# Placing the rounding of the second MLP's weights and the splits of the experts' weights behind the steps they are traced in

## The chip, the cores and the metric

One core of a Trainium2 chip. The metric is the device time of one execution in microseconds (us); lower is better. The engines named below are TensorE (PE; its weight loads are PEld), VectorE (DVE), ScalarE (ACT), GpSimd (POOL) and SyncE (SP, which here only issues DMAs).

## The reference

Attention whose scores are factored, a mixture of experts over its output, and a second MLP over that. 8 x 576 = 4608 tokens of width 512; 8 experts of inner width 1024, two for each token; the second MLP has inner width 2048 and the activation h cos h.

```python
k_s = softmax(k, over the sequence); kv = einsum('bhsd,bhse->bhde', k_s, v)
x = einsum('bhsd,bhde->bhse', softmax(q, over d), kv)        # 4608 x 512
noisy = x @ w_gate + log1p(exp(x @ w_noise)) * noise
top2 of noisy per token, with softmax weights
y = sum over the two experts e of weight * (relu(x @ w1[e]) @ w2[e])
h = y @ w_in; out = ((h * cos(h)) @ w_out) as float32
```

The inputs w_in and w_out of the second MLP come as float64 and are handed to the kernel as pairs of 32-bit words.

## The kernel before

The kernel is written against a tile framework that traces instructions in program order and then orders each engine's queue by a simulation of its own: an instruction is queued when it is ready there, and earlier program order goes first among the ready ones. The engines run their queues strictly in that order. `tc.issue_after(ins)` adds an edge that is about order alone: what the block traces on the engine of `ins` stands behind `ins` in that engine's queue. Each `tc.If` (the block for an expert's tenth block of tokens, `last_block`, line 698) is ordered as one unit.

**Stages.** Attention runs in 36 columns of 128 tokens (`x_unit`); columns 18 to 35 stand in the second half of the main body and share their time with the routing (`routing`, in three chunks), the loading of expert 0's weights and, from column 26, the first groups of expert 0 (`early_group`). Then `experts()` (line 885) walks over `steps`, pairs of a token group g and a slice f of 128 inner columns. Expert 0 has groups of 2, 2, 2 and 3 blocks of 128 tokens (groups 0 to 2 are the early ones, group 3 the first in `experts()`), experts 1 to 7 groups of 4, 3 and 2 blocks, 8 slices each, so 24 steps; then come nine groups of 4 blocks with 16 slices for the second MLP.

**One step.** Matrix products are made in a split form, a = hi + lo, in three products. `mm1` (line 745) makes ph = x @ w1 for one slice; ScalarE writes hh, the rounded relu of ph, and VectorE hl = relu(ph) - hh (line 757). For the second MLP a chain of eight instructions takes the place of the relu (`times_cos`). `mm2`, LAG = 2 steps later, multiplies hh and hl with w2 into an accumulator per block. After a group's last slice the accumulators are copied to ys, even ones by ScalarE, odd ones by VectorE (line 787), and stored. The list `after` holds every hl in the order of tracing; `prep`, which transposes the next group's gathered rows on VectorE (line 677) and splits them into xh and xl (lines 680, 681), is already queued behind the hl of its step by it.

**Background work** is written as generators that are advanced by some steps at fixed places. `wbg` runs `w_load(e)` (line 125): 16 pieces of 128x512, of each a DMA into one of three buffers wst, a copy hi on ScalarE (line 136) and a subtraction lo on GpSimd (line 137); two sets of weights alternate. `cbg` runs `convert()` (line 810): 64 jobs, 32 for w_in and 32 for w_out, each of which loads 128x256 float64 numbers (line 844), makes float32 numbers of them by eight VectorE instructions (lines 821 to 825 as half1, 831 to 833 as half2) and stores them to DRAM (line 834), with two load buffers c64. It is added at the last step of group 3 and must be done by the end of expert 6, since expert 7's time loads the second MLP's first half. `nxt` is the next group, nx its blocks to prepare, p0 the step at which their preparation starts. A wait of SP, VectorE or another engine holds all that is behind it in its queue.

Of the kernel before, what the change touches and what calls it, by code (L numbers as in the profile page):

```python
# [10 lines left out]
F32 = mybir.dt.float32  # L11
# [16 lines left out]
def tile_attention_moe_moe2(  # L28
# [85 lines left out]
        return res  # L114

    W = [None, None]

    def alloc_w(pool, i):
        w1h = pool.tile([P, NK, F], F32R, name=f"w1h{i}")
# [5 lines left out]
    def w_load(e):  # L125

        pend = []
        w1h, w1l, w2h, w2l = W[e % 2]

        def split():  # L130
            (kind, i, fh, _), st = pend.pop(0)
            if kind == 0:
                hi, lo = w1h[:, i, fh * 512:(fh + 1) * 512], w1l[:, i, fh * 512:(fh + 1) * 512]
            else:
                hi, lo = w2h[:, i, :], w2l[:, i, :]
            nc.scalar.activation(hi, st, AF.Copy)  # L136
            nc.gpsimd.tensor_tensor(lo, st, hi.bitcast(F32), op=ALU.subtract)  # L137

        for pc in w_pieces(e):
            st = late[0].tile([P, 512], F32, name="wst", bufs=3)  # L140
            nc.sync.dma_start(st, pc[3])
            pend.append((pc, st))
            if len(pend) == 3:
                yield
                split()
        while pend:
            yield
            split()
# [209 lines left out]
    def x_t(n):  # L358

        t, c9 = divmod(n, PC)  # L360
        pt = ps_at("pqt", "tr", 2)
        for i in range(4):
            if c9 < 8:
                b, c = 2 * t + c9 // 4, c9 % 4
                src = QE[2 * b + i // 2][:, c, 2 * (i % 2):2 * (i % 2) + 2, :]
            else:
                src = QTL[t][:, 2 * i:2 * i + 2, :]
            nc.tensor.transpose(pt[:, i * P:(i + 1) * P], src.rearrange("p h d -> p (h d)"), ident)
        qtt = at.tile([P, 4, P], F32, name="qtt", bufs=2)
        nc.scalar.activation(qtt, pt.rearrange("p (i s) -> p i s", i=4), AF.Exp)  # L370
        QTT[n] = qtt

    def x_mm(n):
# [324 lines left out]
    def last_block(g):  # L698
# [4 lines left out]
        def up(f):  # L703
            fs = slice(f * P, (f + 1) * P)
            ph = ps_tr("ph")
            hh, hl = HH[f % (LAG + 1)][:, LASTB], HL[f % (LAG + 1)][:, LASTB]
            t = GB[f % 2][:, :P]
            if g.nb == 2:
                for kc in range(NK):
                    nc.tensor.matmul(ph[:, :2 * P], w1h[:, kc, fs], g.xh[:, kc, 2 * P:], start=kc == 0, stop=False)  # L710
                    nc.tensor.matmul(ph[:, :P], w1l[:, kc, fs], g.xh[:, kc, 2 * P:3 * P], start=False,
                                     stop=kc == NK - 1)
                nc.scalar.activation(t, ph[:, P:2 * P], AF.Copy)
                nc.vector.tensor_tensor(t, ph[:, :P], t, op=ALU.add)
            else:
                for kc in range(NK):
                    nc.tensor.matmul(ph[:, :P], w1h[:, kc, fs], g.xh[:, kc, LASTB], start=kc == 0, stop=False)
                    nc.tensor.matmul(ph[:, :P], w1h[:, kc, fs], g.xl[:, kc, LASTB], start=False, stop=False)
                    nc.tensor.matmul(ph[:, :P], w1l[:, kc, fs], g.xh[:, kc, LASTB], start=False, stop=kc == NK - 1)
                nc.vector.tensor_copy(t, ph[:, :P])  # L720
            nc.scalar.activation(hh, t, AF.Relu)
            nc.vector.scalar_tensor_tensor(hl, t, 0.0, hh.bitcast(F32), op0=ALU.max, op1=ALU.subtract)
            hs.append((hh, hl))
# [21 lines left out]
    def mm1(g, f):  # L745
# [7 lines left out]
        j = steps.index((g, f)) % (LAG + 1)  # L753
        hh, hl = HH[j][:, :g.N], HL[j][:, :g.N]
        if g.t is None:
            nc.scalar.activation(hh, ph, AF.Relu)  # L756
            after.append(nc.vector.scalar_tensor_tensor(hl, ph, 0.0, hh.bitcast(F32), op0=ALU.max, op1=ALU.subtract))  # L757
        else:
            kk = late[1].tile([P, 512], F32, name="kk", bufs=2)
            r = late[1].tile([P, 512], F32, name="r", bufs=2)  # L760
            times_cos(r, kk, ph)
            nc.scalar.activation(hh, r, AF.Copy)  # L762
            after.append(nc.vector.tensor_tensor(hl, r, hh.bitcast(F32), op=ALU.subtract))  # L763
        HT[g.i, f] = (hh, hl)

# [42 lines left out]
    EMAX = float(2 ** 16 * (1 + 7 / 8 - 2.0 ** -23))  # L808

    def convert():  # L810
        pend = []
        V = nc.vector

        def half1():
            src, t, dst = pend[0]
            v2 = t.rearrange("p (n w) -> p n w", w=2)
            lo, hi = v2[:, :, 0].bitcast(U32), v2[:, :, 1]
            ab = late[1].tile([P, CW], I32, name="ca", bufs=3)
            bits = late[1].tile([P, CW], I32, name="cb", bufs=1)

            V.tensor_single_scalar(ab, hi, 0x7fffffff, op=ALU.bitwise_and)
            V.tensor_scalar(ab.bitcast(F32), ab.bitcast(F32), EMIN, EMAX, op0=ALU.max, op1=ALU.min)
            V.tensor_scalar(bits, ab, 5, 2, op0=ALU.logical_shift_left, op1=ALU.logical_shift_right)
            V.scalar_tensor_tensor(bits, ab, 0x40000000, bits, op0=ALU.bitwise_and, op1=ALU.bitwise_or)
            V.scalar_tensor_tensor(bits, hi, -2 ** 31, bits, op0=ALU.bitwise_and, op1=ALU.bitwise_or)
            return lo, bits, ab

        def half2(lo, bits, ab):
            dst = pend.pop(0)[2]
            w = ab.bitcast(F32)  # L830
            V.tensor_single_scalar(ab, bits, -2 ** 23, op=ALU.bitwise_and)
            V.scalar_tensor_tensor(w, lo, 2.0 ** -52, w, op0=ALU.mult, op1=ALU.mult)
            V.tensor_tensor(w, w, bits.bitcast(F32), op=ALU.add)
            nc.sync.dma_start(dst, w)

        jobs = []
        for src, dst in ((w_in, wi_d), (w_out, wo_d)):
            s32 = src.bitcast(I32)
            for r in range(0, src.shape[0], P):
                for c in range(0, src.shape[1], CW):  # L840
                    jobs.append((s32[r:r + P, 2 * c:2 * (c + CW)], dst[r:r + P, c:c + CW]))
        for src, dst in jobs:
            t = late[1].tile([P, 2 * CW], I32, name="c64", bufs=2)
            nc.sync.dma_start(t, src)
            pend.append((src, t, dst))
            if len(pend) == 2:
                yield
                z = half1()
                yield
                half2(*z)  # L850
        yield
        half2(*half1())

    C2 = 2.0 * math.pi - C1
    MAGIC = 1.5 * 2.0 ** 23
# [29 lines left out]
    def experts():  # L885
# [4 lines left out]
        for i in range(first, len(steps) + LAG):  # L890
# [34 lines left out]
            if nxt is not None and f >= p0:  # L925
# [3 lines left out]
                next(pbg, None)  # L929
                if f == g.nf - 1:  # L930
                    finish(pbg)
            wbg.step(2 if g.t is not None or g.e == 0 else 1)
            if g.nb > 2 or f < p0:
                cbg.step(2 if f == 0 else 1)
            if f == g.nf - 1 and nxt is not None:
                if nxt.t == 0:
                    cbg.drain()
# [73 lines left out]
    for n in range(n, NCOL):  # L1011
# [10 lines left out]
                if t + 1 < NPAIR:  # L1022
                    load_tail(t + 1, "q")
        x_unit(n)
        wbg.step(4)
        if n >= 27:
            bg.step(2)
            dbg.step(1 + n % 2)
# [27 lines left out]
    left = 0  # L1056
    while dbg.q:
        dbg.step()
        left += 1
        if left >= 3:  # L1060
            next(pg, None)
# [93 lines left out]
```

## Time and profile before

| | us |
|---|---|
| median of 3 runs | 1932.73 |
| lowest and highest | 1931.42 and 1937.19 |
| the profiled execution | 1936.69 |
| its span, first to last instruction | 1934.6 |

| engine | busy us | share of the span |
|---|---|---|
| TensorE, matrix products | 1815.6 | 94% |
| TensorE, weight loads | 1531.3 | 79% |
| VectorE | 1118.6 | 58% |
| ScalarE | 860.6 | 44% |
| GpSimd | 447.7 | 23% |

The profile is of one execution. Times in it count from its first instruction; busy time is the union of an engine's instructions, and the granted clock is the share of full speed that TensorE was given. A wait names the engine and instruction that stood, and what ended the wait.

### The profile page before, as it was taken

The page shows a single profiled execution, that of the slowest core. Times are in us where ns is not written, and L with a number is a line of the kernel's source. Part 1 is how long each engine was busy: PE and PEld are TensorE (multiplying, and loading weights), DVE is VectorE, ACT ScalarE, POOL GpSimd, SP SyncE. Part 2 cuts the span into 40 slices and gives each one's busy share as a digit, 9 for nine tenths or more (in the row PEclk, how much of TensorE's full clock was granted, in tenths as well). Part 3 has the DMA queues.
Part 4 walks back from the last instruction along what each step waited for, and adds up shares of the span by engine and source line. Part 5 has one row for each costly group of instructions (what it writes and reads, how often), then busy time and mean ns, then how long its engine had stood idle before and what let it go on. Part 6 is the DMA issues. An engine that isn't in the chain of part 4 may idle for free. (4 is left out here: it accounts for less than half of the span.)

```text
span 1934.6 us, 27003 instructions
## 1 busy us (share of the span) xinstructions
PE 1815.6 (94%) x9738; PEld 1531.3 (79%) x9738; DVE 1118.6 (58%) x2138; ACT 860.6 (44%) x1514; POOL 447.7 (23%) x405
## 2 busy tenths in 40 slices
PE   5875988999899999999999999999999999999998
PEld 4764877788787788888888878888888888888886
DVE  4657677877767744334323357665656566665654
ACT  5542223313123132232424256666666666666654
POOL 6655033404114023041405143110101010110000
PEclk8775999999999999999999999999999999999999
DMA  9954246546545443252435342211212030201000
GB/s 269 291 168 129 79 128 206 186 142 192 150 125 182 141 132 115 79 155 81 133 92 148 98 139 65 71 28 60 56 33 66 23 88 16 72 28 49 1 23 23
DMA packets 179774, 206.18 MB, mean 107 GB/s; under 512 B 34224, under 2 KB 121264, under 8 KB 179632
## 3 DMA queue, kind: packets, MB, share of 16 engines
q1 hardware_dynamic: 160704, 152.17, 26.4%
q0 software_dynamic: 12160, 39.86, 7.1%
q10 hardware_dynamic: 6768, 12.32, 1.7%
q8 instruction: 82, 1.34, 0.3%
q14 instruction: 60, 0.49, 0.1%
HBM read 127.06 MB, written 49.43 MB: 91 GB/s over the span
## 5 line engine op out<-in xcount | busy, mean ns | idle before, releaser
L750 PE MATMUL ph<-xh,w1h 128*128 128x512 f32 (+2 forms) x1376 | 491.9, 357 | 6.9 <-DVE r L696 2.9
L752 PE MATMUL ph<-xh,w1l 128*128 128x512 f32 (+2 forms) x1376 | 491.3, 357 | 0.0
L751 PE MATMUL ph<-xl,w1h 128*128 128x512 f32 (+2 forms) x1376 | 490.6, 357 | 0.0
L774 PE MATMUL acc<-w2h,hh 128*128 128x512 f32 x1152 | 455.8, 396 | 17.1 <-DVE ys L787 9.7
L775 PE MATMUL acc<-w2l,hh 128*128 128x512 f32 x1152 | 453.3, 394 | 0.0
L776 PE MATMUL acc<-w2h,hl 128*128 128x512 f32 x1152 | 427.7, 396 | 21.5 <-DVE hl L757 19.7
L750 PEld LDWEIGHTS ph<-xh,w1h 128*128 128x128 f32 x1376 | 261.8, 190 | 47.1 <-DVE hl L757 4.0
L751 PEld LDWEIGHTS ph<-xl,w1h 128*128 128x128 f32 x1376 | 261.5, 190 | 38.2 <-DMA xl<-xg 0.8
L752 PEld LDWEIGHTS ph<-xh,w1l 128*128 128x128 f32 x1376 | 261.8, 190 | 32.1
L776 PEld LDWEIGHTS acc<-w2h,hl 128*128 128x128 f32 x1152 | 217.2, 190 | 73.7 <-DVE hl L757 26.1
L774 PEld LDWEIGHTS acc<-w2h,hh 128*128 128x128 f32 x1152 | 218.2, 189 | 65.7 <-ACT hh L756 11.1
L775 PEld LDWEIGHTS acc<-w2l,hh 128*128 128x128 f32 x1152 | 218.4, 190 | 40.4
L757 DVE SCALAR_TENSOR_TENSOR hl<-ph,hh 128x256 fp32r<-128x256 f32 (+2 forms) x200 | 107.1, 538 | 243.3 <-ACT hh L756 243.1
L756 ACT ACTIVATE hh<-ph 128x256 fp32r<-128x256 f32 (+2 forms) x200 | 93.9, 472 | 265.2 <-PE ph L752 250.8
L696 DVE SCALAR_TENSOR_TENSOR r<-r,ph 128x512 f32<-128x512 f32 x144 | 98.9, 687 | 151.4 <-ACT r L695 150.3
L618 POOL DMA_INDIRECT xg<-x_d,idx x80 | 76.8, 959 | 441.8 <-DVE xl L681 190.4
L694 ACT ACTIVATE r<-r 128x512 f32<-128x512 f32 x144 | 90.7, 630 | 151.9 <-DVE r L693 151.9
L763 DVE TENSOR_TENSOR hl<-r,hh 128x512 fp32r<-128x512 f32 x144 | 102.1, 709 | 86.4 <-ACT hh L762 86.3
L680 ACT ACTIVATE xh<-xg 128x512 fp32r<-128x512 f32 x106 | 66.7, 630 | 166.2 <-DVE xg L677 164.0
L137 POOL TENSOR_TENSOR w1l<-wst,w1h 128x512 fp32r<-128x512 f32 x80 | 104.9, 1326 | 137.9 <-ACT w1h L136 137.0
L618 POOL DMA_INDIRECT xg<-y_d,SL x36 | 34.3, 954 | 420.5 <-DVE xl L681 389.8
L692 DVE SCALAR_TENSOR_TENSOR r<-kk,ph 128x512 f32<-128x512 f32 x144 | 98.7, 685 | 51.6 <-ACT kk L691 50.0
(186 smaller groups left out, 2162.9 us busy)
## 6 DMA issues: line engine op xcount, KB each, us to landing
wst<-in_moe_w_dram SPq DMA_DIRECT2D x128, 256.0 KB
xl<-xg SPq DMA_DIRECT2D x396, 64.0 KB
y_d<-ys ACTq DMA_DIRECT2D x47, 256.0 KB
kt<-in_k_dram SPq DMA_DIRECT2D x16, 512.0 KB
vt<-in_v_dram SPq DMA_DIRECT2D x16, 512.0 KB
qt<-in_q_dram SPq DMA_DIRECT2D x16, 512.0 KB
x_d<-xs SPq DMA_DIRECT2D x32, 256.0 KB
c<-in_moe_w_in_dram SPq DMA_DIRECT2D x32, 256.0 KB
```

The costliest lines, as they stand in the source:

```text
L137: nc.gpsimd.tensor_tensor(lo, st, hi.bitcast(F32), op=ALU.subtract)
L618: return nc.gpsimd.indirect_dma_start(out=dst, out_offset=None, in_=src, in_offset=bass.IndirectOffsetOnAxis(ap=ix, axis=0))
L692: nc.vector.scalar_tensor_tensor(r, kk, -C1, ph, op0=ALU.mult, op1=ALU.add)
L696: nc.vector.scalar_tensor_tensor(r, r, 1.0, ph, op0=ALU.subtract, op1=ALU.mult, reverse0=True)
L750: nc.tensor.matmul(ph, w1h[:, kc, fs], g.xh[:, kc, :g.N], start=kc == 0, stop=False)
L751: nc.tensor.matmul(ph, w1h[:, kc, fs], g.xl[:, kc, :g.N], start=False, stop=False)
L752: nc.tensor.matmul(ph, w1l[:, kc, fs], g.xh[:, kc, :g.N], start=False, stop=kc == NK - 1)
L757: after.append(nc.vector.scalar_tensor_tensor(hl, ph, 0.0, hh.bitcast(F32), op0=ALU.max, op1=ALU.subtract))
L763: after.append(nc.vector.tensor_tensor(hl, r, hh.bitcast(F32), op=ALU.subtract))
L774: nc.tensor.matmul(g.acc[m], hh[:, ms], w2h[:, fr, :], start=f == 0, stop=False)
L775: nc.tensor.matmul(g.acc[m], hh[:, ms], w2l[:, fr, :], start=False, stop=False)
L776: nc.tensor.matmul(g.acc[m], hl[:, ms], w2h[:, fr, :], start=False, stop=f == g.nf - 1)
```

## The change

Rounding jobs are cut into four pairs of instructions, each queued behind the newest hl, with `cbg` stepping by pairs (1 to 3 a step) where it stepped by half jobs. Loads run three jobs ahead, the third buffer being GB[0], a gather buffer of the second MLP that is not yet in use; `last_block` keeps its scratch in GB[1] alone. A job's store is issued after the next job's first pair. The copy hi of a weight split is queued behind the newest entry of a new list `behind`: the hh of a step, or in the attention columns the exponential that writes qtt. Columns 18 and up advance `wbg` by 2 where they did by 4, steps of expert 0's group 3 by 1 where they did by 2, and the loop that finishes the early groups now advances it by 1.

```diff
--- before.py
+++ after.py
@@ -114,6 +114,7 @@
         return res
 
     W = [None, None]
+    behind = []
 
     def alloc_w(pool, i):
         w1h = pool.tile([P, NK, F], F32R, name=f"w1h{i}")
@@ -133,7 +134,9 @@
                 hi, lo = w1h[:, i, fh * 512:(fh + 1) * 512], w1l[:, i, fh * 512:(fh + 1) * 512]
             else:
                 hi, lo = w2h[:, i, :], w2l[:, i, :]
-            nc.scalar.activation(hi, st, AF.Copy)
+
+            with tc.issue_after(behind[-1].ins):
+                nc.scalar.activation(hi, st, AF.Copy)
             nc.gpsimd.tensor_tensor(lo, st, hi.bitcast(F32), op=ALU.subtract)
 
         for pc in w_pieces(e):
@@ -367,7 +370,7 @@
                 src = QTL[t][:, 2 * i:2 * i + 2, :]
             nc.tensor.transpose(pt[:, i * P:(i + 1) * P], src.rearrange("p h d -> p (h d)"), ident)
         qtt = at.tile([P, 4, P], F32, name="qtt", bufs=2)
-        nc.scalar.activation(qtt, pt.rearrange("p (i s) -> p i s", i=4), AF.Exp)
+        behind.append(nc.scalar.activation(qtt, pt.rearrange("p (i s) -> p i s", i=4), AF.Exp))
         QTT[n] = qtt
 
     def x_mm(n):
@@ -704,7 +707,7 @@
             fs = slice(f * P, (f + 1) * P)
             ph = ps_tr("ph")
             hh, hl = HH[f % (LAG + 1)][:, LASTB], HL[f % (LAG + 1)][:, LASTB]
-            t = GB[f % 2][:, :P]
+            t = GB[1][:, f % 2 * P:f % 2 * P + P]
             if g.nb == 2:
                 for kc in range(NK):
                     nc.tensor.matmul(ph[:, :2 * P], w1h[:, kc, fs], g.xh[:, kc, 2 * P:], start=kc == 0, stop=False)
@@ -753,13 +756,13 @@
         j = steps.index((g, f)) % (LAG + 1)
         hh, hl = HH[j][:, :g.N], HL[j][:, :g.N]
         if g.t is None:
-            nc.scalar.activation(hh, ph, AF.Relu)
+            behind.append(nc.scalar.activation(hh, ph, AF.Relu))
             after.append(nc.vector.scalar_tensor_tensor(hl, ph, 0.0, hh.bitcast(F32), op0=ALU.max, op1=ALU.subtract))
         else:
             kk = late[1].tile([P, 512], F32, name="kk", bufs=2)
             r = late[1].tile([P, 512], F32, name="r", bufs=2)
             times_cos(r, kk, ph)
-            nc.scalar.activation(hh, r, AF.Copy)
+            behind.append(nc.scalar.activation(hh, r, AF.Copy))
             after.append(nc.vector.tensor_tensor(hl, r, hh.bitcast(F32), op=ALU.subtract))
         HT[g.i, f] = (hh, hl)
 
@@ -808,48 +811,58 @@
     EMAX = float(2 ** 16 * (1 + 7 / 8 - 2.0 ** -23))
 
     def convert():
-        pend = []
         V = nc.vector
-
-        def half1():
-            src, t, dst = pend[0]
-            v2 = t.rearrange("p (n w) -> p n w", w=2)
-            lo, hi = v2[:, :, 0].bitcast(U32), v2[:, :, 1]
-            ab = late[1].tile([P, CW], I32, name="ca", bufs=3)
-            bits = late[1].tile([P, CW], I32, name="cb", bufs=1)
-
-            V.tensor_single_scalar(ab, hi, 0x7fffffff, op=ALU.bitwise_and)
-            V.tensor_scalar(ab.bitcast(F32), ab.bitcast(F32), EMIN, EMAX, op0=ALU.max, op1=ALU.min)
-            V.tensor_scalar(bits, ab, 5, 2, op0=ALU.logical_shift_left, op1=ALU.logical_shift_right)
-            V.scalar_tensor_tensor(bits, ab, 0x40000000, bits, op0=ALU.bitwise_and, op1=ALU.bitwise_or)
-            V.scalar_tensor_tensor(bits, hi, -2 ** 31, bits, op0=ALU.bitwise_and, op1=ALU.bitwise_or)
-            return lo, bits, ab
-
-        def half2(lo, bits, ab):
-            dst = pend.pop(0)[2]
-            w = ab.bitcast(F32)
-            V.tensor_single_scalar(ab, bits, -2 ** 23, op=ALU.bitwise_and)
-            V.scalar_tensor_tensor(w, lo, 2.0 ** -52, w, op0=ALU.mult, op1=ALU.mult)
-            V.tensor_tensor(w, w, bits.bitcast(F32), op=ALU.add)
-            nc.sync.dma_start(dst, w)
-
         jobs = []
         for src, dst in ((w_in, wi_d), (w_out, wo_d)):
             s32 = src.bitcast(I32)
             for r in range(0, src.shape[0], P):
                 for c in range(0, src.shape[1], CW):
                     jobs.append((s32[r:r + P, 2 * c:2 * (c + CW)], dst[r:r + P, c:c + CW]))
-        for src, dst in jobs:
-            t = late[1].tile([P, 2 * CW], I32, name="c64", bufs=2)
-            nc.sync.dma_start(t, src)
-            pend.append((src, t, dst))
-            if len(pend) == 2:
-                yield
-                z = half1()
-                yield
-                half2(*z)
-        yield
-        half2(*half1())
+        ring, loads, store = [], itertools.count(), None
+
+        def load():
+            n = next(loads)
+            if n < len(jobs):
+
+                t = GB[0].bitcast(I32) if n % 3 == 2 else late[1].tile([P, 2 * CW], I32, name="c64", bufs=2)
+                nc.sync.dma_start(t, jobs[n][0])
+                ring.append(t)
+
+        def held():
+
+            return tc.issue_after(after[-1].ins)
+
+        for _ in range(3):
+            load()
+        yield
+        for _, dst in jobs:
+            v2 = ring.pop(0).rearrange("p (n w) -> p n w", w=2)
+            lo, hi = v2[:, :, 0].bitcast(U32), v2[:, :, 1]
+            ab = late[1].tile([P, CW], I32, name="ca", bufs=3)
+            bits = late[1].tile([P, CW], I32, name="cb", bufs=1)
+            w = ab.bitcast(F32)
+
+            with held():
+                V.tensor_single_scalar(ab, hi, 0x7fffffff, op=ALU.bitwise_and)
+                V.tensor_scalar(w, w, EMIN, EMAX, op0=ALU.max, op1=ALU.min)
+            yield
+            if store is not None:
+                nc.sync.dma_start(*store)
+            with held():
+                V.tensor_scalar(bits, ab, 5, 2, op0=ALU.logical_shift_left, op1=ALU.logical_shift_right)
+                V.scalar_tensor_tensor(bits, ab, 0x40000000, bits, op0=ALU.bitwise_and, op1=ALU.bitwise_or)
+            yield
+            with held():
+                V.scalar_tensor_tensor(bits, hi, -2 ** 31, bits, op0=ALU.bitwise_and, op1=ALU.bitwise_or)
+                V.tensor_single_scalar(ab, bits, -2 ** 23, op=ALU.bitwise_and)
+            yield
+            with held():
+                V.scalar_tensor_tensor(w, lo, 2.0 ** -52, w, op0=ALU.mult, op1=ALU.mult)
+                V.tensor_tensor(w, w, bits.bitcast(F32), op=ALU.add)
+            store = (dst, w)
+            load()
+            yield
+        nc.sync.dma_start(*store)
 
     C2 = 2.0 * math.pi - C1
     MAGIC = 1.5 * 2.0 ** 23
@@ -929,9 +942,10 @@
                 next(pbg, None)
                 if f == g.nf - 1:
                     finish(pbg)
-            wbg.step(2 if g.t is not None or g.e == 0 else 1)
-            if g.nb > 2 or f < p0:
-                cbg.step(2 if f == 0 else 1)
+            wbg.step(2 if g.t is not None else 1)
+
+            busy = f < LAG or (nxt is not None and p0 <= f < p0 + nxt.nx)
+            cbg.step((1 if g.nb == 2 or f < LAG else 2) if busy else 2 if g.nb == 2 else 3)
             if f == g.nf - 1 and nxt is not None:
                 if nxt.t == 0:
                     cbg.drain()
@@ -1022,7 +1036,7 @@
                 if t + 1 < NPAIR:
                     load_tail(t + 1, "q")
         x_unit(n)
-        wbg.step(4)
+        wbg.step(2)
         if n >= 27:
             bg.step(2)
             dbg.step(1 + n % 2)
@@ -1056,6 +1070,7 @@
     left = 0
     while dbg.q:
         dbg.step()
+        wbg.step()
         left += 1
         if left >= 3:
             next(pg, None)
```

## Rows read from the trace of the kernel before

**Rows 1.** The page's busy time: engine, us, share of the span, instructions.

```profile
PE 1815.6 (94%) x9738; PEld 1531.3 (79%) x9738; DVE 1118.6 (58%) x2138; ACT 860.6 (44%) x1514; POOL 447.7 (23%) x405
```

**Rows 2.** Windows: stretch, length, busy PE PEld DVE ACT POOL, clock, DMA share, GB/s.

```profile
134.00:165.00 31.00, 12.71 (x119) 10.58 (x120) 17.96 (x55) 12.46 (x26) 22.73 (x18) 0.56 0.47 145
165.00:185.00 20.00, 14.29 (x99) 12.03 (x97) 19.66 (x50) 1.79 (x3) 7.29 (x6) 0.50 0.25 83
260.00:334.10 74.10, 61.87 (x332) 53.55 (x331) 55.96 (x110) 23.42 (x45) 33.17 (x29) 0.95 0.62 204
337.70:453.00 115.30, 106.11 (x506) 89.96 (x505) 88.14 (x191) 29.69 (x56) 29.69 (x25) 0.96 0.53 164
453.00:566.60 113.60, 104.18 (x502) 88.39 (x503) 87.09 (x191) 29.20 (x55) 30.22 (x26) 0.97 0.55 165
579.60:694.20 114.60, 105.07 (x506) 88.55 (x505) 82.43 (x188) 29.66 (x56) 29.55 (x25) 0.97 0.52 160
707.20:804.70 97.50, 97.50 (x496) 85.16 (x496) 34.99 (x49) 30.60 (x56) 29.12 (x26) 1.00 0.39 118
1130.00:1160.00 30.00, 25.67 (x101) 19.56 (x101) 13.75 (x16) 18.78 (x33) 19.28 (x17) 0.94 0.60 174
1720.00:1760.00 40.00, 40.00 (x178) 33.15 (x177) 27.78 (x42) 26.84 (x45) 6.08 (x6) 1.00 0.25 72
```

**Rows 3.** Waits, 337 to 694: total us, times, longest us.

```profile
PE acc L776 <- DVE hl L757: 14.6, 11, 2.2
...
PE acc L774 <- DVE ys L787: 9.7, 3, 3.7
```

**Rows 4.** Waits of PE, 260 to 334.1.

```profile
PE acc L776 <- DVE hl L757: 5.2, 2, 3.5
PE acc L774 <- ACT hh L756: 3.1, 3, 1.7
PE ph L750 <- DVE hl L757: 2.7, 3, 1.4
```

**Rows 5.** Waits, whole span, of a rounding job's first instruction.

```profile
DVE ca L821 <- DMA c<-in_moe_w_out_dram: 33.9, 23, 5.4
...
DVE ca L821 <- DMA c<-in_moe_w_in_dram: 29.6, 17, 5.6
```

**Rows 6.** Timeline of VectorE, 479 to 485: start, us, instruction.

```profile
479.66 3.31 DVE L824 SCALAR_TENSOR_TENSOR cb<-ca,cb 128x256 int32<-128x256 int32 x1
483.01 1.43 DVE L825 SCALAR_TENSOR_TENSOR cb<-c,cb 128x256 int32<-128x256 int32 x1
484.36 0.68 DVE L757 SCALAR_TENSOR_TENSOR hl<-ph,hh 128x512 fp32r<-128x512 f32 x1
```

**Rows 7.** Timeline of ScalarE, 479 to 485.

```profile
479.52 0.58 ACT L756 ACTIVATE hh<-ph 128x512 fp32r<-128x512 f32 x1
```

**Rows 8.** Timeline of GpSimd, 479 to 485.

```profile
480.15 1.29 POOL L137 TENSOR_TENSOR w1l<-wst,w1h 128x512 fp32r<-128x512 f32 x1
481.40 1.28 POOL L137 TENSOR_TENSOR w2l<-wst,w2h 128x512 fp32r<-128x512 f32 x1
```

**Rows 9.** Windows, line 821 alone: one instruction per rounding job.

```profile
260.00:334.10 74.10, 3.25 (x10) 0.95 0.62 204
453.00:566.60 113.60, 5.32 (x18) 0.97 0.55 165
```

**Rows 10.** Windows, line 757 alone: one hl per step, group of 3 blocks.

```profile
758.50:779.50 21.00, 2.79 (x5) 1.00 0.15 41
```

**Rows 11.** Instruction groups by line: count, busy us, mean ns.

```profile
L677 DVE STREAM_TRANSPOSE xg<-xl 128x512 f32<-128x512 f32 x99 | 110.7, 1118 | 0.0
...
L681 DVE TENSOR_TENSOR xl<-xg,xh 128x512 fp32r<-128x512 f32 x99 | 72.4, 732 | 30.7 <-ACT xh L680 30.4
```

**Rows 12.** Waits, 134 to 165.

```profile
PE pqt L368 <- ACT qtt L370: 16.5, 5, 4.9
```

**Rows 13.** Waits of SP's queue, 337 to 694.

```profile
SPq L844 <- DVE ca L832: 105.6, 31, 7.4
```

## The prediction

> **What bounds the kernel now.** The page comes first: TensorE is busy 94% of the span [rows 1], so only time in which it stands or runs slowly can be won. An average over the span hides where that is, so I cut it into windows at the branches of the conditional blocks, one window per expert [rows 2]. Seven lines matter. The three experts from 337.7 to 694.2 take 115.3, 113.6 and 114.6 us; the expert at 707.2 does the same 24 steps in 97.5 us with PE at 97.5 of 97.5 and full clock (the next three, not shown, agree within 0.1 us). The slow three differ from it in one thing: VectorE is busy 82 to 88 us there, 35 us in the clean one. That is the rounding of w_in and w_out, 18 of its 64 jobs in each slow expert [rows 9]. Together they lose 343.5 - 3 x 97.5 = 51.0 us, and their clock of 0.96 to 0.97 is inside that sum. Before them, from 260 to 334.1, PE stands 74.1 - 61.9 = 12.2 us, with ten jobs in the window [rows 2, 9].
>
> The waits say by what. In the slow experts PE waits 14.6 us for hl and 9.7 us for the copies ys of finished accumulators, both on VectorE [rows 3]; in 260 to 334.1 for hl 5.2 + 2.7 us and for hh 3.1 us [rows 4]. (The rest of the 51 us is the slow clock and PE's own stops behind those.) VectorE itself stood 33.9 + 29.6 = 63.5 us in front of the first instruction of a rounding job because its load had not landed [rows 5]; everything behind it in that queue stood too. The timeline shows the other half: hh was started at 479.52 and took 0.58 us [rows 7], but its hl ran at 484.36, after two rounding instructions of 3.31 and 1.43 us [rows 6]. So hl was ready to run for over 4 us and the queue order, not the data, held it.
>
> **Rounding behind hl, three buffers.** The work is unchanged: 64 jobs of 8 instructions. A job costs (88.14 - 34.99) / 18 = 2.95 us of VectorE, waits for GpSimd included [rows 2, 9]; a pair 0.74 us. What changes is place. Counted from the new step numbers, an expert takes 17 pairs in its group of 4 blocks, 17 in that of 3 and 10 in that of 2: 44 pairs, 11 jobs. The first two pairs come at the last step of group 3 and the last in expert 6's group of 3 blocks. So the 260 to 334.1 window loses all ten jobs, experts 1 to 3 go from 18 to 11 jobs, and experts 4 to 6, which are clean now, get 11 each.
>
> VectorE then has 35.0 + 11 x 2.95 = 67.5 us of work in 97.5 us, 69%. Is that a limit? By row, no: in 1720 to 1760 VectorE is busy 27.8 of 40 us, also 69%, and PE 40.0 of 40 at full clock [rows 2]. The load before was not only 76%: with the 63.5 us of load waits, about 1 us a job, some 18 us more per slow expert were blocked, 92%. A load that is two to three jobs ahead (a job every 8.9 us) has 18 us or more to land, while the longest wait for one was 5.6 us long; I cost those waits at nothing from now on.
>
> Locally it is tight. In the three middle steps of a group of 3 blocks VectorE has at most hl 0.68 [rows 6], one transposition and one xl, 1.12 + 0.73 [rows 11], and two pairs, 1.48: 4.0 us against a step of 21.0 / 5 = 4.2 us [rows 10]. If the one split of that step blocks the pair for a whole GpSimd instruction, 1.3 us [rows 8], it is 5.3 us, and three steps run 3.3 us late. LAG = 2 covers this: hl is read only two steps later, 8.4 us. Were that cover gone, 3.3 us would be lost in each of six experts. The ys copies have no such cover; they meet one pair at the first two steps. Bounds for the residue per expert: 0 (the 1720 row) and 17 (the slow experts); nearest is the row of equal load, so I take 2, six times 12 us.
>
> The DMAs: a load is now issued behind the fourth pair, a store behind the next job's first pair. Both are in SP's queue, where loads stood 105.6 us behind VectorE before [rows 13], with weight loads and the transposing transfers of xl behind them; with three buffers that wait moves to a later job, the longest was 7.4 us, and it is inside the 0 to 17. The new scratch place of the conditional block and GB[0] as third buffer add no instruction.
>
> **Splits behind hh or the exponential.** No instruction is added here either. A split's hi waits in ScalarE's queue behind the hh of its step; behind it are only copies for transposed blocks and ys; its lo holds back the gathers on GpSimd by up to one step, 5.4 us, once, which the next group's lead of three steps or more covers. In 260 to 334.1 the second expert's weights now come one piece a step, and the 3.1 us of waits for hh should go as well. I take 10 of the 12.2 us: the hl and hh waits without a little left for start-up.
>
> In the columns from 134 to 165 PE waited 16.5 us for the exponential [rows 12] and VectorE was busy 18.0 of 31.0 us, so up to 13.0 us could be won. But from 165 to 185 VectorE is the limit, 19.7 of 20 us [rows 2], with routing; and at two pieces a column about seven splits move into that stretch, where each may block routing for 1.3 us, 9 us. Bounds -13 and +9; nearer the middle, I take -3. At the hand-over to the second MLP, 1130 to 1160, PE stands 4.3 us; bounds -4 and +4, taken 0.
>
> **A rule against the change.** The row first: one rounding instruction took 3.31 us while GpSimd ran two splits back to back from 480.15 to 482.68 [rows 6, 8]. The Trainium skill, "SBUF — State Buffer", section "Who interferes with whom", says that GpSimd and VectorE share one pair of ports as an exclusive lock, so that one of the two blocks for the other's whole instruction. The trace agrees. By that rule a split and a pair released in the same step would collide each time; the rival on the slower side is that case.
>
> **Sum.** The profiled execution took 1936.69 us (span 1934.6 and 2.1 around it), 4.0 above the median of the runs. 1936.7 - 10 (260 to 334.1) - 51 (experts 1 to 3) + 12 (residue) - 3 (columns) = 1884.7; less the 4.0, **1881 us** for the median. 0.3% (6 us) is what a measurement can tell from no change.
>
> **Rivals.**
> - All of it goes: residue 0, columns -13, window -12.2: 1936.7 - 76.2 - 4.0 = 1856. For it: the 1720 row. Against: ys copies without cover. With it, up to a residue of 0.
> - Half comes back: residue 8 an expert, 48 us: 1917. For it: SP's queue still waits for VectorE, and the pairs sit in front of ys.
> - No change: the loss goes with jobs, not with their order. 64 jobs cost 61 us now and would cost 61 again: 1930. Against: the 4 us hold of a ready hl.
> - Slower: split against pair. If each of an expert's 16 splits meets a pair and holds it for its 1.3 us [rows 8], VectorE has 67.5 + 20.8 = 88.3 us, as many as the slow experts have, and all six lose 17: 1936.7 - 10 - 51 - 3 + 102 - 4.0 = 1971. It turns slower once an expert loses over 64 / 6 = 10.7 us. Against: the slow experts' 88 us contain the same 16 splits already, and their VectorE also stood for loads.
>
> **Chances.** Forecast 0.54, all 0.15, half 0.17, no change 0.06, slower 0.08. Faster 0.86, same 0.06, slower 0.08. The range from 1850 to 1926 leaves out the last two and little else.
>
> **What will show it.** No rounding instruction before the last step of group 3; first-of-job waits on the load near zero; experts 1 to 6 alike at 98 to 101 us, clock 1.00, VectorE near 67 us each; no PE wait on hl over 1 us; rounding until about 950 us. Wrong if experts 4 to 6 lose over 10 us each, if ys or hl still end PE's waits, if L833 still has instances of 3 us in numbers, or if the columns to 185 us take longer.

## The result and the profile after

The changed kernel takes 1875.22 us (median of four runs, 1874.38 to 1877.24) where the kernel before takes 1933.51 (four runs): a ratio of 0.9698 [0.9684, 0.9713], 3.0% faster. The forecast was 1881 and faster. The profiled execution took 1874.38 us and its span is 1872.4, so 62.2 us of the span went. The lines named here stand three further down in the changed kernel, up to the rounding: hl is L760, hh L759, the splits' hi and lo L139 and L140; the eight rounding instructions are L846, L847, L852, L853, L856, L857, L860 and L861.

The windows of the changed kernel, cut at the branches of the conditional blocks as in [rows 2] (length, then busy PE, PEld, DVE, ACT, POOL, granted clock, DMA share, GB/s):

```profile
134.00:165.00 31.00, 16.35 (x174) 13.45 (x172) 25.33 (x68) 10.57 (x23) 19.61 (x16) 0.66 0.41 120
165.00:185.00 20.00, 13.13 (x94) 11.03 (x95) 18.73 (x46) 4.47 (x9) 8.43 (x7) 0.59 0.34 110
250.00:318.60 68.60, 66.62 (x399) 59.26 (x396) 26.04 (x65) 22.50 (x46) 28.58 (x28) 1.00 0.49 156
321.20:419.40 98.20, 98.05 (x497) 85.24 (x497) 70.15 (x135) 30.96 (x58) 32.53 (x28) 1.00 0.57 172
422.00:519.60 97.60, 97.45 (x494) 84.85 (x494) 69.49 (x133) 29.32 (x55) 30.15 (x26) 1.00 0.51 159
534.60:632.20 97.60, 97.60 (x497) 85.20 (x496) 70.57 (x136) 29.92 (x56) 30.00 (x26) 1.00 0.51 158
647.10:744.80 97.70, 97.70 (x498) 85.29 (x497) 70.69 (x136) 29.92 (x56) 30.00 (x26) 1.00 0.51 158
872.30:969.80 97.50, 97.50 (x496) 85.14 (x496) 63.57 (x119) 29.82 (x56) 30.06 (x26) 1.00 0.47 145
```

The third row ends where expert 1's first conditional block starts; it has no rounding in it. The next five are experts 1, 2, 3, 4 and 6. The first three were 115.3, 113.6 and 114.6 us; all five are now what only the clean experts were, with PE busy in nearly the whole stretch at a granted clock of 1.00 while VectorE is busy about 70 us (63.6 in expert 6), twice the 35 us of the clean expert of before.

Where the 62.2 us went, from the branch that ends a stretch to the one that ends the next, profiled execution against profiled execution:

| stretch | before, us | after, us | difference |
|---|---|---|---|
| columns, up to the early groups' hl | | | -1.1 |
| from there to the end of group 3 | | | -14.4 |
| both: start to the end of group 3 | 334.1 | 318.6 | -15.5 |
| experts 1, 2, 3 | 118.1, 114.4, 114.5 | 100.8, 100.2, 97.6 | -48.5 |
| the two conditional blocks behind experts 1 to 3 in which PE works | 13.0, 13.0 (26.0 together) | 14.9, 14.9 (29.9 together) | +3.9 |
| second MLP, last branch to the end | 804.6 | 802.4 | -2.2 |

These make -62.3; experts 4 to 6 differ by 0.1 us in all.

Now the waits. In the whole stretch from 321 to 970, experts 1 to 6, TensorE's matrix products have no row at all among the waits; its weight loads have three (us in total, times, longest):

```profile
PEld acc L779 <- issue: 0.5, 1, 0.5
PEld acc L779 <- DVE cb L853: 0.5, 1, 0.5
PEld ph L754 <- issue: 0.5, 2, 0.3
```

The 14.6 us for hl and the 9.7 us for ys of [rows 3] have no successor. What stands is VectorE, in the same stretch:

```profile
DVE hl L760 <- ACT hh L759: 151.5, 107, 5.8
DVE gb L717 <- ACT gb L716: 27.9, 20, 3.7
...
DVE ys L790 <- PE acc L779: 5.4, 11, 1.0
```

The sign has turned round: hl used to be ready and stand behind rounding; now VectorE has finished its background work and stands 107 times at hl, waiting for hh. No wait for a rounding load is left among VectorE's rows. Such idle time costs nothing: VectorE is off the path.

One step as it now runs, VectorE from 442.9, then ScalarE and GpSimd (start, us, instruction; idle time before it in brackets):

```profile
442.98 0.69 DVE L760 SCALAR_TENSOR_TENSOR hl<-ph,hh 128x512 fp32r<-128x512 f32 x1 [1.96 <-ACT hh L759]
443.59 1.11 DVE L680 STREAM_TRANSPOSE xg<-xl 128x512 f32<-128x512 f32 x1
444.61 0.44 DVE L852 TENSOR_SCALAR cb<-ca 128x256 int32<-128x256 int32 x1
445.08 0.43 DVE L853 SCALAR_TENSOR_TENSOR cb<-ca,cb 128x256 int32<-128x256 int32 x1
```

```profile
442.35 0.60 ACT L759 ACTIVATE hh<-ph 128x512 fp32r<-128x512 f32 x1 [2.47 <-PE ph L755]
442.84 0.62 ACT L139 ACTIVATE w1h<-wst 128x512 fp32r<-128x512 f32 x1
```

```profile
443.60 1.30 POOL L140 TENSOR_TENSOR w1l<-wst,w1h 128x512 fp32r<-128x512 f32 x1 [1.35 <-DMA wi_d<-ca]
```

VectorE waits 1.96 us and runs hl 0.03 us after hh has ended at 442.95. Then come a transposition and a rounding pair. The split's copy hi stands behind the hh of its step, so GpSimd's one subtraction starts after hl is nearly done.

That spacing shows in the rounding as well, here in an instruction with two inputs (L824 before, L853 after) and one with one input (L831, L857). First the kernel before, then the changed one (shortest/median/longest ns, first and last start):

```profile
L824 DVE SCALAR_TENSOR_TENSOR cb<-ca,cb x64: 370/426/3314, 265.8 to 692.6; 128x256 int32<-128x256 int32 x64
L831 DVE TENSOR_SCALAR ca<-cb x64: 252/289/4440, 267.1 to 694.0; 128x256 int32<-128x256 int32 x64
```

```profile
L853 DVE SCALAR_TENSOR_TENSOR cb<-ca,cb x64: 417/426/1399, 321.3 to 945.7; 128x256 int32<-128x256 int32 x64
L857 DVE TENSOR_SCALAR ca<-cb x64: 280/294/296, 328.0 to 947.6; 128x256 int32<-128x256 int32 x64
```

The medians are the same within 5 ns; the instances of 3 to 4 us are gone (for the 3.31 us, [rows 8] show two splits in a row). The longest, 1.40 us, is about one split. Collisions have not become fewer: 34 of the 512 rounding instructions took over 0.6 us before, up to 4.44 us, and 60 do now, up to 1.40 us, each beside a split; what has changed is that none lasts longer than about one split, and that they stand behind hl. The rounding is spread from 318 to 949 us instead of 265 to 707.

### The profile page after: what moved, and what is told of

Read it like the earlier page. It is cut to its first block, busy times and chain, and to the rows that moved or that the text cites. A ratio compares the mean times of both kernels' runs of the same rounds, so it can differ in the third digit from the quotient of the medians.

```text
span 1872.4 us, 27040 instructions
## 1 busy us (share of the span) xinstructions
PE 1798.1 (96%) x9738; PEld 1525.2 (81%) x9738; DVE 1136.9 (61%) x2138; ACT 857.8 (46%) x1514; POOL 452.4 (24%) x405
## 5 line engine op out<-in xcount | busy, mean ns | idle before, releaser
L779 PE MATMUL acc<-w2h,hl 128*128 128x512 f32 x1152 | 422.1, 391 | 0.6
L759 ACT ACTIVATE hh<-ph 128x256 fp32r<-128x256 f32 (+2 forms) x200 | 95.6, 478 | 392.2 <-PE ph L755 387.6
L760 DVE SCALAR_TENSOR_TENSOR hl<-ph,hh 128x256 fp32r<-128x256 f32 (+2 forms) x200 | 108.1, 541 | 247.0 <-ACT hh L759 238.7
L140 POOL TENSOR_TENSOR w1l<-wst,w1h 128x512 fp32r<-128x512 f32 x80 | 106.1, 1329 | 258.0 <-ACT w1h L139 241.5
L140 POOL TENSOR_TENSOR w2l<-wst,w2h 128x512 fp32r<-128x512 f32 x80 | 106.6, 1337 | 134.2 <-ACT w2h L139 106.2
```

What stands on the lines that cost most here:

```text
L779: nc.tensor.matmul(g.acc[m], hl[:, ms], w2h[:, fr, :], start=False, stop=f == g.nf - 1)
```

## The experiments

Theory A: what the 51 us of experts 1 to 3 cost was order alone, hl and ys standing behind rounding in VectorE's queue, and the order edge removes it whatever the load. The rivals: the load (18 jobs an expert against 11, so density), the waits for the loads (so the third buffer), the splits' collisions. Each kernel was timed beside the kernel before; ratios carry their 95% interval.

### The two parts apart

rounding_alone keeps the new `convert`, its pace and buffers, and frees the splits again:

```diff
-            with tc.issue_after(behind[-1].ins):
-                nc.scalar.activation(hi, st, AF.Copy)
+            nc.scalar.activation(hi, st, AF.Copy)
...
-            wbg.step(2 if g.t is not None else 1)
+            wbg.step(2 if g.t is not None or g.e == 0 else 1)
...
-        wbg.step(2)
+        wbg.step(4)
...
-        wbg.step()
```

> The changed kernel with the rounding's part alone: pairs behind hl, three buffers, the new pace; the splits are free again, 4 a column, 2 a step in expert 0, none in the loop that finishes the early groups. Theory A, order: it is the rounding ahead of a ready hl that stopped TensorE, so experts 1 to 6 stay at 97.5 to 98.5 us and nearly all of the 58 us is here: 1875 to 1883 us, the rest being what the splits do before expert 1. Theory B, the splits count as much: free copies on ScalarE that wait for their load hold hh, so experts 1 to 3 are at 101 us or more and the total is 1890 us or more.

Measured: 1883.36 us, 0.9736 [0.9718, 0.9755]. Expert 1 in it:

```profile
325.00:423.10 98.10, 97.95 (x498) 85.12 (x497) 66.00 (x133) 30.17 (x56) 30.26 (x26) 1.00 0.49 159
```

Clean: nearly all of the gain is the rounding part.

splits_alone is the other half: `convert`, its pace and the conditional block's scratch of before, with the splits held and their new pace.

> The kernel before with the splits' part alone: hi behind hh or the exponential, 2 a column, 1 a step in expert 0 and in the loop that finishes the early groups. The rounding is as before. Theory A, order of the rounding: experts 1 to 3 keep losing 14 us or more each, total 1922 to 1936 us. Theory B: hh comes sooner and hl with it, experts 1 to 3 win 5 us or more each, total 1915 us or less.

Measured: 1944.39 us, 1.0047 [1.003, 1.0065]: slower by half a per cent, outside of what was expected. (Its profiled execution, 1937.89 us, is the fastest of five, so its rows show less than the median lost.) Its experts 1 and 2, and PE's first wait from 328 to 570 (9.1 us from 337 to 580 before):

```profile
327.50:448.20 120.70, 107.87 (x505) 90.31 (x505) 90.40 (x181) 29.99 (x58) 32.96 (x28) 0.94 0.50 160
450.40:569.60 119.20, 105.69 (x500) 89.08 (x501) 96.55 (x198) 27.70 (x55) 29.17 (x25) 0.96 0.50 159
```

```profile
PE acc L779 <- DVE hl L760: 23.2, 12, 4.7
```

The early part gained 9.8 of the 15.5 us that the whole change gains there (expert 1 starts at 324.3 instead of 334.1), and the three experts then lost more than that, 14 us. So beyond the early part the splits' edge gained nothing while hl still stood behind rounding.

### The hold, the pace and the buffers

no_hold is the changed kernel without the rounding's order edge alone:

```diff
         def held():
-            return tc.issue_after(after[-1].ins)
+            return ExitStack()
```

> The changed kernel with the pairs traced at the same steps and with three buffers, but with no order edge behind hl, so that the ordering may queue them as soon as they are ready. Theory A, order: pairs are queued ahead of hl again and packed into the first experts, whose windows go back to 108 us or more: total 1915 to 1935 us. Rival, pace and buffers: the three buffers and the finer steps are what helped; waits for loads stay near zero, experts stay under 101 us, total 1875 to 1890 us.

Measured: 1928.78 us, 0.9963 [0.995, 0.9976]. Windows of its experts 1 and 2 and PE's waits from 326 to 570:

```profile
326.00:447.70 121.70, 107.32 (x505) 89.60 (x504) 97.08 (x204) 29.70 (x58) 32.63 (x28) 0.94 0.54 170
450.00:568.50 118.50, 104.34 (x501) 87.77 (x501) 100.10 (x213) 28.23 (x55) 29.66 (x25) 0.97 0.53 168
```

```profile
PE acc L779 <- DVE hl L760: 24.4, 14, 4.4
PE acc L777 <- DVE ys L790: 3.0, 1, 3.0
```

With loads three jobs ahead and pairs in place of halves, VectorE stood 2.3 us for a load in that stretch (and 24.9 us for stores), and these two experts lost as much as ever. So neither the buffer nor the cut does it.

three_pairs_a_step keeps the hold and packs the work: `cbg.step(3)` in every step, 17, 18 and 17 jobs in experts 1 to 3, nearly as many as before.

> The changed kernel with three pairs at every step, so 18 jobs an expert as in the kernel before, and rounding done within the first four experts; pairs still behind hl, three buffers. VectorE then has about 35 + 18 x 3.2 = 93 us of work in 97.5 us. Theory A, order: hl goes ahead and LAG covers the rest, experts 1 to 3 at 100 us or less, total within 8 us of the changed kernel, 1875 to 1883. Rival, density: what helped is that only 11 jobs fall into an expert; with 18 the windows go back to 108 us or more and the total to 1905 us or more.

Measured: 1874.77 us, 0.9691 [0.9673, 0.9708], as the changed kernel. Its experts 1 to 3:

```profile
321.00:419.80 98.80, 98.65 (x500) 85.78 (x499) 80.68 (x179) 30.51 (x58) 32.47 (x27) 1.00 0.61 194
422.00:520.60 98.60, 98.60 (x499) 85.95 (x500) 83.09 (x187) 28.86 (x55) 30.05 (x25) 1.00 0.60 189
534.20:632.40 98.20, 98.20 (x500) 85.69 (x499) 84.66 (x188) 29.64 (x56) 29.95 (x25) 1.00 0.60 190
```

VectorE is busy up to 84.66 of 98.20 us, 86%, and PE does not stop. In [rows 2] it was busy 76% and PE lost 17 us. Density falls as a rival.

hold_alone is the kernel before with one edge around each half of a job and nothing else:

```diff
+            mark = tc.issue_after(after[-1].ins)
+            mark.__enter__()
             V.tensor_single_scalar(ab, hi, 0x7fffffff, op=ALU.bitwise_and)
...
+            mark.__exit__(None, None, None)
             return lo, bits, ab
...
+            mark = tc.issue_after(after[-1].ins)
+            mark.__enter__()
             V.tensor_single_scalar(ab, bits, -2 ** 23, op=ALU.bitwise_and)
...
+            mark.__exit__(None, None, None)
             nc.sync.dma_start(dst, w)
```

> The kernel before with one thing added: each half of a rounding job (five instructions, three instructions) is queued behind the newest hl. Two load buffers, the old pace of 22 halves an expert, free splits. Theory A, the order edge is the gain: experts 1 to 6 at 97.5 to 100 us, the total that of the rounding's part alone, 1878 to 1890 us. Rival, the cut into pairs and the third buffer carry it: halves of 1.8 us in front of the next hl and jobs that wait for loads in the queue, experts at 103 us or more, 1900 us or more.

Measured: 1882.53 us, 0.9735 [0.972, 0.975], the same as rounding_alone. The edge alone makes the whole of the rounding part's gain, with two buffers, halves and the old pace. That pace was in the program all along: the rounding ran ahead of it, as early as its loads allowed, 18 jobs an expert and done by 707, and behind hl it falls back to 11 jobs an expert and runs until 948 (no_hold, where nothing keeps it, has 21 in experts 1 and 2 each). VectorE's waits for the loads, 57.8 us from 321 to 707 before, shrink to this one row:

```profile
DVE ca L823 <- DMA c<-in_moe_w_in_dram: 0.7, 1, 0.7
```

They were a result of that running ahead. What they cost by themselves while hl stood behind them, no run separates from the order.

two_buffers takes the third buffer from the changed kernel:

```diff
-                t = GB[0].bitcast(I32) if n % 3 == 2 else late[1].tile([P, 2 * CW], I32, name="c64", bufs=2)
+                t = late[1].tile([P, 2 * CW], I32, name="c64", bufs=2)
...
-        for _ in range(3):
+        for _ in range(2):
             load()
```

> The changed kernel with two load buffers in place of three, loads two jobs ahead. Theory A, order: an expert has 11 jobs, one in about 9 us, and a load lands in time or its wait stands behind hl where nothing waits for it; 1873 to 1880 us. Rival, loads: about 1 us of wait a job comes back and stands in VectorE's queue ahead of the next hl and of ys, experts at 101 us or more, 1890 us or more.

Measured: 1873.73 us, 0.9684 [0.9669, 0.9699]: the buffer is worth nothing.

edges_only is hold_alone with the splits' edge added, the paces of before:

```diff
+    behind = []
...
-            nc.scalar.activation(hi, st, AF.Copy)
+            with tc.issue_after(behind[-1].ins):
+                nc.scalar.activation(hi, st, AF.Copy)
...
```

> The kernel before with the two order edges and nothing else: rounding halves behind the newest hl, splits' hi behind hh or the exponential. Two buffers, halves, the old places and numbers of steps for both. Theory A, order is the whole change: 1871 to 1879 us, as the changed kernel. Rival: the splits' new step numbers (2 a column, one a step in expert 0, and in the loop that finishes the early groups) are part of it; then expert 1 starts later than in the changed kernel and the total stays at 1880 us or more.

Measured: 1877.74 us, 0.971 [0.969, 0.973]. Two order edges make about 56 of the 58 us that the medians differ by.

### The columns

columns_4 goes back to four splits a column, `wbg.step(4)`, held as in the change.

> The changed kernel with four splits a column, still behind the exponential, so that they are done by column 22, before the routing's VectorE work. If the splits that fall into the routing are what gave back the 8.6 us that the columns had won by column 22, the columns end 3 to 6 us earlier: 1869 to 1873 us. If splits in front of the next exponential wait for their loads as before, the win by column 22 is gone and the total is 1875 to 1880 us.

Measured: 1878.84 us (1873.99 to 1881.82), 0.9713 [0.9699, 0.9726]; its interval overlaps that of the changed kernel, and the 3 to 6 us that the first expectation hoped for did not come. From 134 to 170 PE waits for the exponential nearly as long as before the change [rows 12]:

```profile
PE pqt L371 <- ACT qtt L373: 12.9, 5, 4.8
```

columns_gap moves the splits instead: three a column up to column 20, none from 21 to 25, then two, `wbg.step(3 if n < 21 else 0 if n < 26 else 2)`.

> The changed kernel with three splits a column up to column 20, none from 21 to 25, where the routing's first chunk keeps VectorE busy, and two a column after. If splits on GpSimd in that stretch hold the routing's VectorE instructions, early groups start 3 to 7 us earlier and so does the end: 1868 to 1872 us. If the routing itself is the limit there, nothing moves: 1873 to 1877 us.

Measured: 1874.47 us (1866.97 to 1878.12), 0.9683 [0.966, 0.9707]. From column 23 to 28 the columns run 7 to 8 us ahead of the kernel before (6 us ahead of the changed kernel at column 28), and by columns 32 to 35 only 0.6 to 2.2 us are left of it. So the total decides for neither expectation. PE's wait for routing from 165 to 185, 10.2 us in the changed kernel, is 3.6 us here. Why the columns from 29 on give it back was not found.

### What the splits have to do with it

before_no_lo is the kernel before, with GpSimd's subtraction replaced by a write of zeros, so that GpSimd reads nothing; the low parts of the experts' weights are left out of the result, the same matrix products are made.

```diff
-            nc.gpsimd.tensor_tensor(lo, st, hi.bitcast(F32), op=ALU.subtract)
+            nc.gpsimd.memset(lo.bitcast(F32), 0.0)
```

> The kernel before with the splits' subtraction on GpSimd left out: lo is filled with zeros, which reads nothing (so the products with lo contribute nothing to the output). Theory A, order: rounding stays ahead of hl, and experts 1 to 3 still lose most of their 14 to 17 us each, 1915 us or more. Rival, the splits on GpSimd that stretch rounding instructions are the loss: without them no rounding instruction is over 2 us, experts 1 to 3 fall to 102 us or less, 1890 us or less.

Measured: 1903.91 us, 0.9843 [0.9819, 0.9868], between the two expectations. Its experts 1 to 3, and the two-input rounding instruction (ns as above):

```profile
325.00:434.30 109.30, 102.75 (x506) 87.85 (x505) 82.31 (x191) 29.60 (x56) 16.08 (x25) 0.98 0.55 173
436.90:543.30 106.40, 101.30 (x500) 87.10 (x501) 81.38 (x188) 27.66 (x52) 15.58 (x25) 0.98 0.55 175
556.30:662.90 106.60, 101.73 (x506) 88.01 (x505) 74.31 (x183) 30.05 (x56) 9.78 (x12) 0.98 0.53 169
```

```profile
L824 DVE SCALAR_TENSOR_TENSOR cb<-ca,cb x64: 378/425/437, 263.3 to 653.7; 128x256 int32<-128x256 int32 x64
```

The longest instance falls from 3314 to 437 ns, and the three experts lose 322.3 - 3 x 97.5 = 29.8 us instead of 51.0. So theory A, as stated, is too narrow: 21 us of the 51 go with the subtractions, most likely as rounding instructions that splits had stretched while hl stood behind them; 30 us are lost without any subtraction. GpSimd is not quite out of those 30 us either. The zeros wait for no load, so all 16 of an expert are written in a row, and in experts 1 and 2 they held a rounding instruction with one input, L823, for 7.32 and 7.44 us; PE's waits for the hl behind them were 1.0 and 1.2 us.

splits_no_lo makes the same replacement in splits_alone, to ask whether its slowdown is such collisions.

> The kernel before with the splits' part alone, and the subtraction on GpSimd replaced by zeros as in the run before_no_lo. The splits' part alone was 9 us slower than the kernel before. If that came from splits and rounding released by the same hh that block each other, it is gone here and this run is no slower than before_no_lo, within 5 us. If it came from the splits' copies or their step numbers, this run is 8 us or more slower than before_no_lo.

Measured: 1911.63 us, 0.9881 [0.9856, 0.9906], 7.7 us above before_no_lo, again between the expectations. PE's two first waits from 323 to 570:

```profile
PE ph L753 <- DVEq L734: 7.9, 1, 7.9
PE acc L779 <- DVE hl L760: 6.6, 6, 2.4
```

One stall of 7.9 us at a conditional block (DVEq is VectorE's sequencer, at the branch) is as long as the whole difference in this execution, and the replacement itself made it (VectorE, GpSimd, PE):

```profile
432.99 8.30 DVE L834 TENSOR_SCALAR ca<-cb 128x256 int32<-128x256 int32 x1
433.61 1.93 POOL L140 MEMSET w1l<- 128x512 f32 x4
441.50 0.77 PE L753 MATMUL ph<-xh,w1h 128*128 128x512 f32 x1 [7.87 <-DVEq L734]
```

A rounding instruction stood 8.30 us beside sixteen writes of zeros in a row (the first four are shown), and VectorE, and PE with it, passed the branch behind it only then. Without that stall the two kernels would be about level. The extra waits for hl are 4 us here (6.6 against 2.4), where they were 14 with the subtractions (23.2 against 9.1). So most of what splits_alone lost in the experts speaks for such collisions, but how the half per cent divides stays open.

None of these kernels is faster than the changed one by more than its interval.

## Why the prediction was right, point by point

**Order, not load (-51).** Right, and the best tested: hold_alone takes the loss away with one edge, no_hold brings it back by taking that edge out, three_pairs_a_step keeps it away at the old density. Branch to branch the three experts gave 48.5 us, 44.6 with the two conditional blocks behind them (below). The prediction put all 51 us down to the order; some 21 of them needed the splits' subtractions as well (before_no_lo). What the prediction drew beside it was wrong in one place: it argued that VectorE "blocked" 92% of the time, load waits included, was what made 76% harmful, and so gave the third buffer and the longer lead a share. The load waits came from the order and went with it (hold_alone), no_hold lost as much in experts 1 and 2 with 2.3 us of them (and 24.9 us for stores), and two_buffers lost nothing.

**Residue (+12).** The term that was most mis-sized. Forecast 2 us an expert; measured against 97.5 us 0 to 0.2 us in experts 2 to 6 and 0.7 in expert 1, about 1 us in all. The local sum, 4.0 us of VectorE in a step of 4.2 and 5.3 with a split, held in its size: VectorE is busy 70 us an expert where 67.5 were forecast. But the cover, LAG = 2, was taken as a maybe; with hl at the head of each step a late pair only shortens VectorE's next wait for hh, 151.5 us long in all. Nor did the waits of SP's queue matter; they went on:

```profile
SPq L828 <- DVE ca L860: 68.0, 28, 9.1
SPq L828 <- DVE ca L846: 66.3, 13, 5.6
```

This is SP from 321 to 970, its loads behind VectorE; nothing of PE's waited for what stood behind them.

**From 260 to the end of group 3 (-10).** Measured -14.4, more than the whole 12.2 us in which PE stood, since the clock came back too: 0.95 in [rows 2], 1.00 from 250 to 318.6. What stands there now is little (PE's waits):

```profile
PE pt L674 <- DMA xg<-x_d,idx: 1.3, 1, 1.3
PE acc L777 <- ACT hh L759: 0.5, 1, 0.5
```

**Columns (-3).** Measured -1.1, with movements both ways, as the prediction had it. In 134 to 165 PE waits 3.8 us for the exponential (16.5 before), and column 22's exponential comes 8.6 us earlier; in 165 to 185, where four splits now start (one before; the prediction had counted seven), PE waits for routing:

```profile
PE ptb L532 <- DVE bl L429: 10.2, 3, 7.9
```

It was 4.7 us before. By column 28 the lead is 1.1 us. That the splits cause it is argued from the place and from columns_gap: with none of them there until 183 us, the wait is 3.6 us and the lead lasts to column 28, to be lost later.

**Second MLP (0).** Measured -2.2. The same stretch takes 804.6 to 806.5 us in the three kernels with free splits (before, hold_alone, rounding_alone) and 799.6 to 803.7 in the eight with held ones, so the edge on the splits that remain there seems to be worth some 2 us (the middle ones are 804.6 and 802.2); that is one execution of each.

**A term that was missing (+3.9).** The two conditional blocks in which PE works behind experts 2 and 3 take 14.9 us where they took 13.0. No time is lost there. The block behind expert 3, first before, then after the change:

```profile
694.20:707.20 13.00, 13.00 (x90) 11.93 (x89) 5.49 (x20) 4.67 (x16) 0.94 (x1) 1.00 0.19 53
632.20:647.10 14.90, 14.90 (x98) 13.50 (x97) 4.80 (x18) 4.67 (x16) 0.78 (x1) 1.00 0.26 75
```

PE is busy all through both, with 90 and 98 matrix products, and expert 3 in front of the block has nearly as many fewer, 506 [rows 2] and now 497. So some 2 us of work changed sides of the branch. The clean expert of [rows 2], with 496, had them in its block already (15.0 us, 99 products); of each slow expert's loss, read against it, some 1 to 2 us were only that. Why the cut falls elsewhere was not tried.

**The sum.** 1881 against 1875.22 is nearer than its terms: of the profiled execution the forecast took 52 us, and 62 went. The residue was 11 us too large and the stretch before expert 1 and the second MLP gave 6.6 us more than forecast, while the columns gave 1.9 us less and the 51 us were about 5 too many. That these partly cancel is luck.

**The rivals.** "All goes" (1856) is right for the residue and wrong for the columns, whose 13 us did not come. "Half comes back" and "no change" fall with three_pairs_a_step. The slower one, split against pair, named a real collision: VectorE is busy 70 us in expert 1 with held splits, 66.0 in rounding_alone with free ones, and 60 rounding instructions are stretched where 34 were. It costs nothing, because what is stretched stands behind hl. In the kernel before it cost, by before_no_lo some 21 us. The prediction's rule of the Trainium skill, "SBUF — State Buffer", section "Who interferes with whom", that one of GpSimd and VectorE blocks for the other's whole instruction, fits the stretched instructions of both kernels: each ends 0.1 to 0.3 us after the end of a split.

## What to carry to other kernels

When a fully busy engine loses time to background work on another one, look in that engine's timeline whether the instruction that is waited for was ready and only stood behind others; if so, one edge about order, background work behind the newest critical instruction, may give back all of it without any work removed, and the engine's occupancy is no measure of the danger (76% lost 17 us an expert, 86% lost 1). Put the edge on the queue whose instruction the path waits for, first: the same sort of edge on a neighbour's queue alone, with its new pace, made this kernel half a per cent slower. Waits for loads in such a trace may be the result of work that ran ahead; try the order before adding buffers.

## What was not expected of the hardware

A GpSimd subtraction with two operands in SBUF stretches some VectorE instructions and leaves others alone. The rounding instruction L824, with two inputs, took up to 3.31 us beside two of them in a row [rows 6, 8], nearly eight times its median, and never over 0.44 us when GpSimd only wrote (before_no_lo). The transposition, with one input, took 1.11 us beside a subtraction of 1.30 us that began with it, its mean of [rows 11]. The Trainium skill, "SBUF — State Buffer", section "Who interferes with whom", says that a VectorE instruction with two SBUF inputs contends with a GpSimd instruction that reads SBUF, and not with one that only writes it. For the rounding instructions with two inputs the trace agrees.

It is not the whole of it, since rounding instructions with one input are held too, by splits and by writes of zeros alike. The longest of the kernel before, beside three splits in a row (VectorE, then GpSimd):

```profile
365.05 4.44 DVE L831 TENSOR_SCALAR ca<-cb 128x256 int32<-128x256 int32 x1
365.53 1.31 POOL L137 TENSOR_TENSOR w1l<-wst,w1h 128x512 fp32r<-128x512 f32 x1
366.78 2.55 POOL L137 TENSOR_TENSOR w2l<-wst,w2h 128x512 fp32r<-128x512 f32 x2
```

It ends at 369.49, 0.16 us after the third split. All rounding instructions over 0.6 us, 34 before the change and 60 after, end so: those with one input, 15 and 30 of them, 0.15 to 0.16 us after the end of a split, those with two 0.28 to 0.29 us after one. The same instructions take 0.29 and 0.43 us at the median. In before_no_lo the two of 7.32 and 7.44 us end 0.15 us after the last of sixteen writes of zeros, which read nothing. What tells a rounding instruction with one input from the transposition, which no split held, was not tried.
